# Recurrent attention and slot mixture of experts on one core: guarded GpSimd products, unnormalised slot inputs, a new order

## The chip, the core and the metric

The kernel runs on one core of a Trainium2 chip. The core has five engines that run beside each other and wait for one another by semaphores: PE (TensorE, matrix products into PSUM, its weight loads listed as PEld), DVE (VectorE), ACT (ScalarE), POOL (GpSimd, which also issues most loads here) and SP (which issues the output). Sixteen DMA engines move data between HBM and SBUF. The metric is the device time of one execution in microseconds (us).

## What is computed

Two layers in a row. The first is a recurrent attention: for each of 4 batches and 8 heads (768 tokens, head width 48) a state of 48 x 48 decays by `w` and takes in the product of key and value at each token. The second mixes all 3072 tokens (width 384) into 32 slots, sends 4 slots to each of 8 experts, and mixes the results back.

```python
for t in range(S):
    cur = np.einsum('bhd,bhe->bhde', u[None] * kt, vt)
    y[:, :, t] = np.einsum('bhd,bhde->bhe', rt, state + cur)
    state = w[None, :, :, None] * state + np.einsum('bhd,bhe->bhde', kt, vt)
...
logits = x @ phi                      # x: y with heads side by side, 3072 x 384
d = softmax(logits over tokens)
slot_input = d.T @ x                  # 32 x 384
slot_out[e] = np.maximum(slot_input[e] @ w1[e], 0.0) @ w2[e]
c = softmax(logits over slots)
out = c @ slot_out
```

## The kernel before

The tokens are cut into 6 chunks of 128 (names carry the chunk c, a pair of batches bl, and a half hf of the heads). For each chunk the kernel turns the raw rows of k, r and v into columns on PE, scales them on the way out of PSUM with tables of powers of w, and computes scores, a diagonal term, the output y (kept as x) and the next state.

Every step is a named task of a small planner (`Plan`, L50): it has an engine, a function, other tasks that must stand ahead of it, and the PSUM banks and buffers that it takes. The table ORDER (L13) lists the tasks in the order in which they are emitted, with the bank numbers behind a colon and, behind a slash, the engine (D, A or P for DVE, ACT, POOL) where there is a choice. Since each engine executes its instructions in the order in which they were emitted, the table sets the order on every engine at once.

The names that matter here:

- `qk`, `qr`, `qv` (L48): a copy of the raw rows into a padded buffer rp, from SBUF to SBUF. `tk`, `tr`, `tv` (L355): transposes on PE. `ek`, `er`, `ev` (L365, or a copy at L201 or L203): eviction, for k and r times a table.
- `bk`, `bv`, `kn`, `vn`: transposes back and their eviction. `A` and `M` (L394, L400): scores on PE, masked on DVE. `pr` (L407): product of k and r; `D`, `ds`: its sums per head. `dv` (L424), on POOL: v times ds. `s`, `S`: state. `Y`, `x`: the output of the recurrence. `X`, `xT`, `l`, `lg`: its transpose and the logits.
- `mx`, `sb`, `ex`, `c`, `cT`: maximum, difference, exponential and transposes for the softmax over slots. `rs`, `rr` (L656): its sums per token and their reciprocals, used when the output is evicted.
- For the softmax over tokens the chunks form three groups g (0 to 2, 3 and 4, 5): `gm`, `gt`, `gr`, `gq`, `gd`, `gb`, `gx` find a running maximum, `gs` subtracts it, `ge` takes the exponential, `dp` (L612) multiplies with x on PE. `gf`, `gg`, `am` give the factor by which the earlier sum `acc` is scaled, `acc` (L616) adds the new one. A row of acc holds the sums of the weights.
- `rc`, `un` (L659, L663): the reciprocal of these sums, and the normalised slot inputs in a padded layout. `h` (L682): products with w1, in two groups of four experts and two halves of the width; `hs` (L691, L693) applies the maximum with zero. `ht`, `hT`: transposes of h. `o` (L709): products with w2, one expert after another, all summed in the bank SO.
- The last expert's w2 comes in two pieces, `Va7` and `Vb7`: with YL = 3 the second has 3 of 8 rows. The first four output tiles don't wait for it: they take what SO holds after the first piece (`so1`), and `gG`, `gE`, `pg` (L762) add the missing rows' part straight from h. The other 20 tiles take `so2`, the whole sum. `p` (L754) is a tile's product, `oe` (L771 on ACT, L773 on DVE) its eviction, `dm` the output transfer of one or several tiles.

Loads are issued from POOL's queue, in among its products: `iL` (36 half pieces of k, r and v), `iW` (8 times w1), `iV` (w2). From the eleventh load on, each waits until the load eight places earlier has landed. They turn float32 into bfloat16 on the way; the first chunk's keys are loaded as float32, one half from SP's queue and one from ACT's.

## Time and profile before

| | us |
|---|---|
| median of 3 runs | 120.48 |
| lowest and highest | 118.22, 120.67 |
| the profiled execution | 118.51 |
| its span, first to last instruction | 116.7 |
| busy in the span: PE, DVE, ACT, POOL | 97.1, 93.4, 75.9, 66.1 |

All times on a row of the profile are those of the profiled execution, counted from the span's start. A row of the timeline has the start, the length, the engine, the line and what is written from what; "x8" says that eight alike stand together, and a bracket tells how long the engine was idle before and what ended the wait. A matmul's end is modelled, so a busy PE isn't a PE at its peak.

### The profile page before, as it was taken

Reading aid. Unit: us, or ns where it says so; the run is one execution under the profiler, and the core shown is the slowest. Engines: PE = TensorE matmul, PEld = TensorE weight load, DVE = VectorE, ACT = ScalarE, POOL = GpSimd, SP = SyncE. Lnnn points to the kernel's source line nnn. Section 1 sums busy time; section 2 is a strip of 40 time slices with the busy share of each in tenths; the row PEclk is TensorE's granted clock in tenths of the full one; section 3 lists DMA queues with packets and bytes.
Section 4 is the critical chain, followed back from the end, with each engine's and each line's share of the span. In section 5 each row is a group of like instructions: output and inputs, shape, how many; then the busy total and the mean of one; then the engine's idle time right before and its main releaser. Section 6 shows DMA issues by size and latency. Waiting matters only on the chain.

```text
span 116.7 us, 3848 instructions
## 1 busy us (share of the span) xinstructions
PE 97.1 (83%) x1624; PEld 75.0 (64%) x1624; DVE 93.4 (80%) x187; ACT 75.9 (65%) x118; POOL 66.1 (57%) x84
## 2 busy tenths in 40 slices
PE   4829999897999999999979999899889959898000
PEld 0329989686988897889958989677564425442000
DVE  6967899999989999999899999997873650299300
ACT  3877399998996899788977872388551060279000
POOL 6935554999899958999998799951210000000000
PEclk9999999999999999999999999999996799999975
DMA  2999999999999999999999999999999993059994
GB/s 34 299 203 207 205 209 206 208 208 206 205 208 218 220 213 216 217 216 208 219 216 215 212 217 215 208 221 216 217 217 211 211 205 66 0 213 394 415 415 181
DMA packets 8992, 25.06 MB, mean 215 GB/s; under 512 B 1168, under 2 KB 5776, under 8 KB 8976
## 3 DMA queue, kind: packets, MB, share of 16 engines
q0 software_dynamic: 7344, 19.27, 84.8%
q1 hardware_dynamic: 1464, 5.16, 11.6%
q10 hardware_dynamic: 168, 0.40, 1.0%
q8 instruction: 12, 0.20, 0.6%
q14 instruction: 4, 0.03, 0.1%
HBM read 39.38 MB, written 4.72 MB: 378 GB/s over the span
## 4 chain that ended last, share of the span: by engine, by line
PE 45%; DVE 30%; issue 7%; DMA 5%; ACT 4%; POOL 1%; ACTq 1%; DVEq 1%; POOLq 0%
DVE AT L400 11%; PE pG L355 10%; PE pG L376 7%; DMA w_all<-in_k_dram 5%; DVE S L453 5%; PE pA L394 4%; PE pG L682 3%; PE pG L754 2%; PE pG L495 2%; PE pG L709 2%; DVE rT L365 2%; PE pG L475 2%; PE pG L469 2%; DVE kT L365 2%; DVE w_all L773 2%
## 5 line engine op out<-in xcount | busy, mean ns | idle before, releaser
L400 DVE TENSOR_TENSOR AT<-pA,mask 128x1024 bf16<-128x1024 f32 x24 | 29.2, 1217 | 0.7 <-PE pA L394 0.6
L201 ACT COPY rp<-raw 128x1536 bf16<-128x1536 bf16 x14 | 20.7, 1487 | 2.8 <-PE pG L355 2.3
L355 PE MATMUL pG<-ident,rp 128*128 128x128 bf16 x288 | 20.7, 230 | 2.1 <-ACT rp L201 2.1
L424 POOL TENSOR_TENSOR dv<-vn,ds 128x768 bf16<-128x768 bf16 x12 | 17.7, 1482 | 4.8 <-ACT ds L201 3.6
L355 PEld LDWEIGHTS <-rp 128*128 128x128 bf16 x288 | 18.1, 103 | 3.0 <-ACT rp L201 2.4
L407 POOL TENSOR_TENSOR pr<-kT,rT 128x1024 bf16<-128x1024 bf16 x8 | 17.1, 2142 | 0.1
L201 ACT CAST x<-pG 128x384 bf16<-128x384 f32 x20 | 9.3, 490 | 4.7 <-PE pG L477 2.6
L394 PE MATMUL pA<-rT,kT 64*128 64x128 bf16 x192 | 9.8, 218 | 1.2 <-DVE AT L400 1.1
L453 DVE TENSOR_TENSOR S<-pG,W 128x384 bf16<-128x384 f32 x20 | 10.4, 547 | 0.0
L201 ACT COPY vT<-pG 128x1024 bf16<-128x1024 bf16 x10 | 10.0, 1023 | 0.5 <-PE pG L355 0.4
L475 PE MATMUL pG<-vn,AT 128*128 128x48 bf16 x192 | 8.7, 183 | 0.0
L773 DVE TENSOR_SCALAR w_all<-pG,rcs 128x384 f32<-128x384 f32 (+1 forms) x13 | 6.9, 596 | 2.2 <-ACT w_all L771 2.2
L394 PEld LDWEIGHTS <-kT 64*128 64x128 bf16 x192 | 5.9, 94 | 4.2 <-issue 3.0
L365 DVE TENSOR_TENSOR kT<-pG,Tk 128x1024 bf16<-128x1024 bf16 x12 | 8.0, 682 | 0.6 <-ACT Tk L309 0.6
L365 DVE TENSOR_TENSOR rT<-pG,Tr 128x1024 bf16<-128x1024 bf16 x12 | 8.1, 683 | 0.3 <-PE pG L355 0.3
L213 POOL DMA_DIRECT2D raw<-in_r_dram x12 | 6.5, 557 | 2.6 <-DMA raw<-in_k_dram 1.8
L213 POOL DMA_DIRECT2D raw<-in_v_dram x12 | 6.3, 531 | 3.0 <-DMA raw<-in_r_dram 3.0
L477 PE MATMUL pG<-dv,ident 128*128 128x384 bf16 x24 | 7.7, 323 | 0.0
L771 ACT ACTIVATE w_all<-pG,rcs 128x384 f32<-128x384 f32 (+1 forms) x12 | 5.8, 586 | 2.7 <-PE pG L762 2.3
L475 PEld LDWEIGHTS <-AT 128*128 128x128 bf16 x192 | 7.1, 96 | 0.2 <-issue 0.2
L201 ACT COPY xT<-pG 128x768 bf16<-128x768 bf16 x7 | 5.6, 800 | 2.5 <-PE pG L495 2.5
L376 PE MATMUL pG<-ident,kT 128*128 128x128 bf16 x80 | 6.2, 237 | 0.9 <-DVE kT L365 0.9
(134 smaller groups left out, 211.6 us busy)
## 6 DMA issues: line engine op xcount, KB each, us to landing
w_all<-in_moe_w_dram POOLq DMA_DIRECT2D x8, 768.0 KB, 19.4
raw<-in_moe_w_dram POOLq DMA_DIRECT2D x7, 768.0 KB, 26.6
out_dram<-w_all SPq DMA_DIRECT2D x5, 768.0 KB, 5.0
raw<-in_r_dram POOLq DMA_DIRECT2D x12, 192.0 KB, 7.1
raw<-in_v_dram POOLq DMA_DIRECT2D x12, 192.0 KB, 7.2
raw<-in_k_dram POOLq DMA_DIRECT2D x10, 192.0 KB, 7.1
raw<-in_moe_w_dram POOLq DMA_DIRECT2D x1, 480.0 KB, 24.4
w_all<-in_k_dram SPq DMA_DIRECT2D x1, 384.0 KB, 4.4
```

The source lines that it names most:

```text
L201: O(act.copy(dst, src))
L213: O(pool.dma_start(out=raw_t(x)[:, bb * JJ * D:(bb + 1) * JJ * D], in_=src[c, bb]))
L355: O(pe.transpose(o[:, :, j, :], rp_r[W[rp]][:, jh * JH + j].rearrange("p b d -> p (b d)"), ident[:]))
L365: O(dve.tensor_mul(dst, src, (Tk, Tr)[which][:, None, jh].to_broadcast(BC)))
L376: O(pe.transpose(bank_b(kb)[:, h * C:(h + 1) * C], src[:, bl, h].rearrange("p a x -> p (a x)"), ident[:]))
L394: O(pe.matmul(pA[:, bb, h4 * C:(h4 + 1) * C], kt[s, bl, h].rearrange("p a x -> p (a x)"), rt[s, bl, h].rearrange("p a x -> p (a x)"), star ...
L400: O(dve.tensor_mul(AT_r[W[f"AT{key}"]][:], pA[:].rearrange("p bb (h t) -> p bb h t", t=C), mask[:, None, None, :].to_broadcast([128, 2, H ...
L407: O(op(e).tensor_mul(pr_r[W[f"pr{c}"]][:, bl], kT_r[W[f"kT{c}"]][:, bl].rearrange("p h j x -> p h (j x)"), rT_r[W[f"rT{c}"]][:, bl].rearra ...
L424: O(op(e).tensor_mul(dv_r[W[f"dv{c}{bl}"]][:], vn_r[W[f"vn{c}{bl}"]][:], ds_r[W[f"ds{c}"]][:, bl, :, :, None].to_broadcast([128, H, 2, D])))
L453: O(dve.tensor_mul(S_r[W[new]][:, s], bank(kb[hf])[:, 0:HD].rearrange("p (h b d) -> p h b d", b=2, d=D), W128[:, s, :, None].to_broadcast( ...
L475: O(pe.matmul(o[:, z:z + D], AT_r[W[at]][:, bb, h4, :], vn[:, hf * H2 + h4, bb, :], start=(c == 0 and h4 == 0 and bb == 0), stop=False, sk ...
L773: O(dve.tensor_scalar(out=dst, in0=src, scalar1=rcs[:, i:i + 1], scalar2=None, op0=ALU.mult))
```

## The change

Eight things are done at once.

1. *Waits of POOL's products.* While emitting, the planner remembers the last DVE instruction of a kind in SHARED (copies of raw rows, products and differences with two SBUF inputs). A task of a kind in HELD that goes to POOL then gets a wait for that instruction (`after`).
2. *Slot inputs unnormalised.* For the last group `un` writes acc plus the bank's new part straight into the padded layout; only the row of sums is added as `acc`. The sums are turned by four small products (`rv`), their reciprocal `hsc` (`rw`) scales h in `hs`.
3. *Start.* Other order of the first loads and settings: POOL makes the index table, the identity and the padding of rp ahead of its first load; DVE no longer sets rp; phi is loaded ahead of u. The keys' two halves come from SP and ACT, as they did.
4. *The first output tile in two banks* (p0a, p0b), so that its halves are evicted from different banks; `so1` is one copy.
5. *Two rows in the last piece of w2* (YL = 2).
6. *Output pieces* of 1, 1, 1, 1, 2, 2 tiles, then 4, 4, then 8.
7. *Extra products* (WARM): 19 products of ones into the scores' bank, behind six named tasks.
8. *A new ORDER*, with other engines for many evictions.

```diff
+WARM = [("gl1", 2), ("gb2", 3), ("dp2", 2), ("o50", 3), ("o60", 6), ("o70", 3)]
+SHARED = ("qk", "qr", "qv", "pr", "dv", "sb", "gd", "gs", "gf", "am")
+HELD = ("pr", "dv", "sb", "gs", "gf", "am")
-zt1 zc iL6 zt3 ze1 iL7 zw:0 zt0 qk00:0/A iL8 za ze3 iL9 zb zt2 qk01:/A iL10 zd:/D ze2 tk00:0,0 ze0 tk01:1 qr0:1/D
...
+zt3 zc iL6 zt1 ze3 iL7 zw:0 zt0 ze1 iL8 zb ze0 iL9 zt2 qk00:0/A za zd:/D ze2 qk01:/D iL10 tk00:0,0 tk01:1 qr0:1/A
...
+        shared = None
         for token in order.split():
...
-            t["fn"](letter.get(e, t["eng"]))
+            e = letter.get(e, t["eng"])
+            t["fn"](e)
+            kind = name.rstrip("0123456789")
+            if e == "DVE" and kind in SHARED and name != "gs2":
+                shared = self.last
+            elif e == "POOL" and kind in HELD and shared is not None:
+                self.after(self.last, shared)
...
+    P = Plan(POOLS)
     def O(ins):
+        P.last = ins
...
+    def after(ins, earlier):
+        tc.add_manual_dep(ins.ins, earlier.ins.name, mybir.DependencyInfo(
+            mybir.DependencyClass.Sync, mybir.DependencyReason.DATA), reason="shared port")
...
-    P = Plan(POOLS)
+    P.after = after
...
-    for bb, eng in enumerate((sp, act)):
-        O(eng.dma_start(out=k0[:, bb * JJ * D:(bb + 1) * JJ * D], in_=k_src[0, bb]))
-    O(sp.dma_start(out=u_r[:, :, 0:D], in_=u[:, None, :].to_broadcast([H, 2, D])))
+    for bb, q in ((0, sp), (1, act)):
+        O(q.dma_start(out=k0[:, bb * JJ * D:(bb + 1) * JJ * D], in_=k_src[0, bb]))
...
+    O(dve.memset(ident_f[:], 0.0))
     for t in (w_r, u_r):
...
-    O(dve.memset(ident_f[:], 0.0))
-    load_rkv(2)
...
+    O(sp.dma_start(out=u_r[:, :, 0:D], in_=u[:, None, :].to_broadcast([H, 2, D])))
+    O(pool.iota(it_i.rearrange("p (j y) -> p j y", j=JJ), pattern=[[-1, JJ], [-JJ, RR]], base=C - 1,
+                channel_multiplier=0))
...
+    for t in rp_r:
+        O(pool.memset(t[:, :, :, D:], 0.0))
+    load_rkv(2)
...
-    O(pool.iota(it_i.rearrange("p (j y) -> p j y", j=JJ), pattern=[[-1, JJ], [-JJ, RR]], base=C - 1,
-                channel_multiplier=0))
...
-    for t in rp_r:
-        O(dve.memset(t[:, :, :, D:], 0.0))
...
-    YL = 3
+    YL = 2
...
-        def mg(e):
-            a = acc[:].rearrange("p m s -> p (m s)")
-            if g:
-                O(dve.tensor_add(a, a, bank(kd)[:, 0:(nM + 1) * ES]))
-            else:
-                O(dve.tensor_copy(a, bank(kd)[:, 0:(nM + 1) * ES]))
-        P.add(f"acc{g}", "DVE", mg, deps=[f"dp{g}"] + ([f"am{g}"] if g else []), use=[kd])
+        if not last:
+            def mg(e):
+                a = acc[:].rearrange("p m s -> p (m s)")
+                if g:
+                    O(dve.tensor_add(a, a, bank(kd)[:, 0:(nM + 1) * ES]))
+                else:
+                    O(dve.tensor_copy(a, bank(kd)[:, 0:(nM + 1) * ES]))
+            P.add(f"acc{g}", "DVE", mg, deps=[f"dp{g}"] + ([f"am{g}"] if g else []), use=[kd])
+        else:
+            for q in range(2):
+                def un(e, q=q):
+                    o = 4 * Spe * q
+                    src = bank(kd)[:, 0:nM * ES].rearrange("p (m s) -> p m s", m=nM)[:, :, o:o + 16]
+                    O(dve.tensor_add(
+                        uns[:, :, q, o:o + 144].rearrange("p m (j x) -> p m j x", x=32 + Spe)[:, :, :, 0:Spe],
+                        acc[:, 0:nM, o:o + 16].rearrange("p m (j x) -> p m j x", j=EG),
+                        src.rearrange("p m (j x) -> p m j x", j=EG)))
+                P.add(f"un{q}", "DVE", un, deps=[f"dp{g}", f"am{g}", "zu"], use=[kd])
+            P.add(f"acc{g}", "DVE", lambda e: O(dve.tensor_add(acc[:, nM, :], acc[:, nM, :],
+                                                               bank(kd)[:, nM * ES:(nM + 1) * ES])),
+                  deps=[f"dp{g}", f"am{g}"], use=[kd])
...
-    csr = sb.tile([128, ES], f32, name="csr")
+    hsc = sb.tile([128, 1], f32, name="hsc")
...
-    P.add("rc", "DVE", lambda e: O(dve.reciprocal(csr[:], acc[:, nM, :])), deps=[f"acc{nG - 1}"])
-    for g in range(2):
-        def un(e, g=g):
-            o = 4 * Spe * g
-            O(op(e).tensor_mul(
-                uns[:, :, g, o:o + 144].rearrange("p m (j x) -> p m j x", x=32 + Spe)[:, :, :, 0:Spe],
-                acc[:, 0:nM, o:o + 16].rearrange("p m (j x) -> p m j x", j=EG),
-                csr[:, o:o + 16].rearrange("p (j x) -> p j x", j=EG)[:, None].to_broadcast([128, nM, EG, Spe])))
-        P.add(f"un{g}", "DVE" if g == 0 else "POOL|DVE", un, deps=["rc", "zu"])
+    def turn_sums(e):
+        for j in range(EG):
+            O(pe.matmul(bank("rvb")[32 * j:32 * j + 32, 0:1], acc[0:1, nM, :], ident_f[0:1, 0:1], start=True, stop=True,
+                        skip_group_check=True))
+    P.add("rv", "PE", turn_sums, deps=[f"acc{nG - 1}"], take=[("rvb", "G")])
+    P.add("rw", "DVE", lambda e: O(dve.reciprocal(hsc[:], bank("rvb")[:, 0:1])), deps=["rv"], use=["rvb"])
...
                 if e == "ACT":
-                    O(act.activation(out=dst, in_=src, func=AF.Relu))
+                    O(act.activation(out=dst, in_=src, func=AF.Relu, scale=hsc[:]))
...
-                    O(dve.tensor_scalar(out=dst, in0=src, scalar1=0.0, scalar2=None, op0=ALU.max))
-            P.add(f"hs{g}{a}", "ACT|DVE", ev, deps=[f"h{g}{a}"], use=[kb])
+                    O(dve.tensor_scalar(out=dst, in0=src, scalar1=hsc[:], scalar2=0.0, op0=ALU.mult, op1=ALU.max))
+            P.add(f"hs{g}{a}", "ACT|DVE", ev, deps=[f"h{g}{a}", "rw"], use=[kb])
...
         P.add(f"gG{y}", "PE", lambda e, y=y, kb=kb: O(pe.matmul(
-            bank(kb), h_sb[1][96:128, nF - YL + y, :], cT[96:128, 0:NE, 0:128], start=True, stop=True)),
+            bank(kb)[:, 0:NE * 128], h_sb[1][96:128, nF - YL + y, :], cT[96:128, 0:NE, 0:128], start=True, stop=True)),
...
-        P.add(f"gE{y}", "ACT|DVE", lambda e, y=y, kb=kb: copy(e, gG[:, y], bank(kb)), deps=[f"gG{y}"], use=[kb])
+        P.add(f"gE{y}", "ACT|DVE", lambda e, y=y, kb=kb: copy(e, gG[:, y], bank(kb)[:, 0:NE * 128]), deps=[f"gG{y}"], use=[kb])
...
             if y0:
-                for x, e_, m0 in (("a", "ACT", 0), ("b", "DVE", Dm // 2)):
-                    P.add(f"so1{x}", e_, lambda e, m0=m0: copy(e, so1[:, m0:m0 + Dm // 2], bank(SO)[:, m0:m0 + Dm // 2]),
-                          deps=[prev], use=[SO])
+                P.add("so1", "DVE", lambda e: copy(e, so1, bank(SO)[:, 0:Dm]), deps=[prev], use=[SO])
...
-                         deps=[f"hT{g}", ld, prev] + (["so1a", "so1b"] if y0 else []), take=[(SO, "G")] if e == 0 else [],
+                         deps=[f"hT{g}", ld, prev] + (["so1"] if y0 else []), take=[(SO, "G")] if e == 0 else [],
...
-    P.add("so2", "DVE", lambda e: copy(e, so2[:], bank(SO)[:, 0:Dm]), deps=[prev], use=[SO])
+    P.add("so2", "ACT|DVE", lambda e: copy(e, so2[:], bank(SO)[:, 0:Dm]), deps=[prev], use=[SO])
...
-    i, last = 0, None
-    for g, sizes in ((0, [1, 1, 2, 4]), (1, [4, 4]), (2, [4, 4])):
+    i, last, pp, pgs = 0, None, [], []
+    for g, sizes in ((0, [1, 1, 1, 1, 2, 2]), (1, [4, 4]), (2, [8])):
...
-                def f(e, g=g, j=j, kb=kb, first=first):
-                    O(pe.matmul(bank(kb)[:, 0:Dm], cT[:, j, g * 128:(g + 1) * 128], so1 if first else so2[:],
-                                start=True, stop=not first))
-                P.add(f"p{i}", "PE", f, deps=(["so1a", "so1b"] if first else ["so2"]) + [f"p{i - 1}" if i else None] + cts,
-                      take=[(kb, "G")])
-                done = f"p{i}"
-                if first:
-                    def f2(e, i=i, kb=kb):
-                        for y in range(YL):
-                            O(pe.matmul(bank(kb)[:, 0:Dm], gG[:, y, i * 128:(i + 1) * 128],
-                                        w2_of(E - 1)[:, nF - YL + y, :], start=False, stop=(y == YL - 1)))
-                    done = P.add(f"pg{i}", "PE", f2, deps=[f"p{i}", f"Vb{E - 1}", f"pg{i - 1}" if i else None] +
-                                 [f"gE{y}" for y in range(YL)], use=[kb])
-                halves = [(0, Dm, "")] if i else [(0, Dm // 2, "a"), (Dm // 2, Dm, "b")]
-                for m0, m1, x in halves:
-                    def ev(e, i=i, kb=kb, m0=m0, m1=m1):
-                        dst, src = obuf[:, i * Dm + m0:i * Dm + m1], bank(kb)[:, m0:m1]
+                halves = [("a", 0, Dm // 2), ("b", Dm // 2, Dm)] if i == 0 else [("", 0, Dm)]
+                for hn, m0, m1 in halves:
+                    def f(e, g=g, j=j, kb=kb + hn, first=first, m0=m0, m1=m1):
+                        O(pe.matmul(bank(kb)[:, 0:m1 - m0], cT[:, j, g * 128:(g + 1) * 128],
+                                    (so1 if first else so2[:])[:, m0:m1], start=True, stop=not first))
+                    pp.append(P.add(f"p{i}{hn}", "PE", f, deps=["so1" if first else "so2"] + pp[-1:] + cts,
+                                    take=[(kb + hn, "G")]))
+                    if first:
+                        def f2(e, i=i, kb=kb + hn, m0=m0, m1=m1):
+                            for y in range(YL):
+                                O(pe.matmul(bank(kb)[:, 0:m1 - m0], gG[:, y, i * 128:(i + 1) * 128],
+                                            w2_of(E - 1)[:, nF - YL + y, m0:m1], start=False, stop=(y == YL - 1)))
+                        pgs.append(P.add(f"pg{i}{hn}", "PE", f2, deps=[f"p{i}{hn}", f"Vb{E - 1}"] + pgs[-1:] +
+                                         [f"gE{y}" for y in range(YL)], use=[kb + hn]))
+                    def ev(e, i=i, kb=kb + hn, m0=m0, m1=m1):
+                        dst, src = obuf[:, i * Dm + m0:i * Dm + m1], bank(kb)[:, 0:m1 - m0]
                         if e == "ACT":
...
-                    names.append(P.add(f"oe{i}{x}", ("ACT", "DVE")[x == "b" or i % 2], ev, deps=[done, "rr"], use=[kb]))
+                    names.append(P.add(f"oe{i}{hn}", "DVE" if hn == "b" or i % 2 else "ACT", ev,
+                                       deps=[(pgs if first else pp)[-1], "rr"], use=[kb + hn]))
...
+    turn_ = ["p0a", "p0b", "p1", "pg0a", "pg0b", "pg1", f"o{E - 1}{nF - YL}", "p2", "pg2", "p3", "pg3", "p4"]
+    for a, b in zip(turn_, turn_[1:]):
+        P.by[b]["deps"].append(a)
     for e in range(E):
...
+    n = 0
+    for after, count in WARM:
+        for x in range(count):
+            P.add(f"F{n}", "PE", lambda e: O(pe.matmul(pA[:, 0, :], ones[:, 0:128], ones[:], start=True, stop=True)),
+                  deps=[after, f"F{n - 1}" if n else None])
+            n += 1
...
```

On POOL the program's start reads so before (raw is the buffer of the loads, w_all here the index table, ident_f the identity):

```order
L213 DMA raw<-in_r_dram 128x1x768
L242 ISA
L242 AFFINE_SELECT ident_f<-ident_f 128x128
L213 DMA raw<-in_r_dram 128x1x768
L245 IOTA w_all 128x128
L213 DMA raw<-in_v_dram 128x1x768 x2
```

and so after:

```order
L262 ISA
L262 IOTA w_all 128x128
L264 AFFINE_SELECT ident_f<-ident_f 128x128
L267 MEMSET rp_77 128x32x16
L267 MEMSET rp_78 128x32x16
L234 DMA raw<-in_r_dram 128x1x768 x2
L234 DMA raw<-in_v_dram 128x1x768 x2
```

Four instructions now stand ahead of the first load.

On POOL, around the first product dv, with the semaphores that each row waits for (DVE_49 is DVE's, Activation_49 ACT's, DMASW those of loads), before:

```order
L213 DMA raw<-in_r_dram 128x1x768 [waits DMASW2_49]
L213 DMA raw<-in_r_dram 128x1x768 [waits DMASW3_49]
L424 TENSOR_TENSOR dv_88<-vn_82,ds_86 128x768 [waits Activation_49]
L213 DMA raw<-in_v_dram 128x1x768 [waits DMASW4_49]
L213 DMA raw<-in_v_dram 128x1x768 [waits DMASW5_49]
```

and after:

```order
L234 DMA raw<-in_v_dram 128x1x768 [waits DMASW4_49]
L445 TENSOR_TENSOR dv_88<-vn_82,ds_86 128x768 [waits DVE_49,Activation_49]
L234 DMA raw<-in_v_dram 128x1x768 [waits DMASW5_49]
L234 DMA raw<-in_k_dram 128x1x768 [waits DMASW6_49]
L234 DMA raw<-in_k_dram 128x1x768 [waits DMASW7_49]
L234 DMA raw<-in_r_dram 128x1x768 [waits DMASW0_49]
```

The product stands one load later and also waits for DVE; the loads behind it wait with it.

On DVE, from the last difference to the slot inputs and h (kT and rT are reused for h and its transpose), before:

```order
L593 TENSOR_TENSOR dd<-lg_all,pG_67 128x128
L588 COPY run_181<-pG_67 128x32
L599 TENSOR_TENSOR fac_189<-run_180,run_181 128x32
L203 COPY cT<-pG_69 128x32x16
L619 TENSOR_TENSOR acc<-acc,pG_68 128x128
L659 RECIPROCAL csr<-acc 128x32
L663 TENSOR_TENSOR uns<-acc,csr 128x3x4x4 x2
L657 RECIPROCAL rcs<-pG_64 128x24
L693 TENSOR_SCALAR kT_71<-pG_65 128x8x64
```

and after:

```order
L609 COPY run_181<-pG_68 128x32
L614 TENSOR_TENSOR dd<-lg_all,pG_68 128x128
L624 TENSOR_TENSOR acc<-acc,fac_189 128x128
L656 TENSOR_TENSOR acc<-acc,pG_64 128x32
L651 TENSOR_TENSOR uns<-acc,pG_64 128x3x4x4 x2
L701 RECIPROCAL hsc<-pG_67 128x1
L727 TENSOR_SCALAR kT_71<-pG_69,hsc 128x8x64
L727 TENSOR_SCALAR kT_70<-pG_65,hsc 128x8x64
```

The factor fac_189 goes to POOL and the scaling of acc comes from POOL to DVE; the copy cT and the reciprocals rcs have left this place.

## What I expect

> **What bounds the kernel now.** I read the stretches first (columns: the stretch in us, busy us and instructions of PE, PEld, DVE, ACT, POOL, then the granted clock, the DMA engines' share, GB/s).
>
> ```profile
> 8.00:80.00 72.00, 68.98 (x1311) 60.16 (x1312) 69.39 (x114) 57.51 (x82) 58.99 (x66) 1.00 1.09 212
> 84.90:88.30 3.40, 2.76 (x67) 2.27 (x63) 2.65 (x12) 1.45 (x4) 0.46 (x1) 1.00 1.04 215
> 88.30:91.70 3.40, 3.32 (x32) 1.25 (x36) 0.88 (x4) 0.60 (x1) 0.00 (x0) 0.50 1.05 217
> ...
> 4.00:94.00 90.00, 83.70 (x1511) 68.51 (x1511) 81.98 (x151) 65.87 (x99) 63.27 (x75) 0.98 1.09 214
> ...
> 102.00:105.00 3.00, 2.89 (x17) 1.43 (x16) 3.00 (x6) 2.21 (x5) 0.00 (x0) 1.00 0.55 204
> 105.00:115.00 10.00, 2.47 (x11) 0.80 (x9) 3.87 (x8) 3.18 (x7) 0.00 (x0) 0.86 1.01 409
> ```
>
> Two things run in parallel. From 8 to 80 us DVE (69.39 of 72) and PE (68.98) leave hardly a gap; that is the chain of waits. But the DMA engines are full from 4 to 94 us as well: the loads stream at 214 GB/s. 105 to 115 is output at 409 GB/s. So I asked when the last weights land and who takes them, in the DMA issues (size, us to landing), the timeline and the chain (start, length, what).
>
> ```profile
> raw<-in_moe_w_dram POOLq DMA_DIRECT2D x1, 480.0 KB, 24.4
> raw<-in_moe_w_dram POOLq DMA_DIRECT2D x1, 288.0 KB, 22.1
> ```
> ```profile
> 73.09 0.59 POOL L219 DMA_DIRECT2D raw<-in_moe_w_dram  x1
> 76.79 0.59 POOL L219 DMA_DIRECT2D raw<-in_moe_w_dram  x1
> ```
> ```profile
> 96.18 2.79 PE pG L709 x61
> 99.00 0.37 DVE vT L203
> 99.39 0.33 ACT vT L201
> 99.76 0.81 PE pG L754 x4
> 100.57 0.50 PE pG L762 x3
> 101.09 0.43 ACT w_all L771
> 101.55 0.94 DVE w_all L773 x2
> ```
> ```profile
> 102.04 7.66 SPq L778 DMA_DIRECT2D out_dram<-w_all  x8
> ```
>
> The last expert's first piece (5 rows of w2) lands at 73.09 + 24.4 = 97.5, its last (3 rows) at 76.79 + 22.1 = 98.9. The products with w2 (L709) begin at 96.18 and end at 98.97. Compute is thus only some 1.2 us behind the weights: had it been early, the five products on the 97.5 piece (5 x 2.79/61 = 0.23) would have ended near 97.75. The serial tail follows: two halves of so1 one after the other, four tiles, three corrections, two halves of tile 0 one after the other, first output issued at 102.04. From there to the span's end at 116.7 it is 14.66 us, nearly all transfer.
>
> **The change part by part.** *Start.* POOL used to issue its first load at once; now iota, select and two memsets of rp stand ahead of it.
>
> ```profile
> 1.25 0.70 POOL L213 DMA_DIRECT2D raw<-in_r_dram  x1 [0.81 <-POOLq L801]
> 1.37 0.62 ACTq L233 DMA_DIRECT2D w_all<-in_k_dram  x1
> 2.82 0.31 POOL L245 IOTA w_all<- 128x128 int32 x1
> 52.81 0.89 POOL L325 MEMSET uns<- 128x960 bf16 x1
> 7.36 0.83 ACT L201 CAST rp<-w_all 128x768 bf16<-128x768 f32 x1 [0.75 <-DMA w_all<-in_k_dram]
> ```
> ```profile
> w_all<-in_k_dram ACTq DMA_DIRECT2D x1, 384.0 KB, 6.0
> raw<-in_r_dram POOLq DMA_DIRECT2D x12, 192.0 KB, 7.1
> ```
>
> Iota and select cost some 0.3 each, a memset of 512 elements 0.89 x 512/960 = 0.47: the first load is issued 0.3 + 0.3 + 0.9 = 1.6 later. That is not a loss of 1.6 in the stream: today the second half of the keys (issued 1.37, landed 7.4) shares the engines with those loads; alone it should land near 6, and what the r loads give up the keys take. I put the stream's end 0.1 late (bounds: 0.3 early, 1.6 late) and the first transposes 1.0 early (0 to 1.7). The two key queues themselves are the same as before.
>
> *Middle.* The table moves evictions. Groups of DVE (count | busy us, mean ns):
>
> ```profile
> L203 DVE COPY xT<-pG 128x768 bf16<-128x768 bf16 x5 | 2.8, 551 | 0.4 <-PE pG L495 0.4
> L203 DVE COPY kn<-pG 128x768 bf16<-128x768 bf16 x5 | 2.7, 548 | 0.2 <-PE pG L376 0.2
> L203 DVE COPY rp<-raw 128x1536 bf16<-128x1536 bf16 x3 | 1.8, 592 | 0.0
> L203 DVE COPY vT<-pG 128x1024 bf16<-128x1024 bf16 x2 | 1.4, 681 | 0.0
> L203 DVE COPY cT<-pG 128x512 bf16<-128x512 bf16 x3 | 1.3, 418 | 0.3 <-PE pG L530 0.3
> ```
>
> DVE loses four kn, two vn of the same width, three xT, three cT: 2.2 + 1.1 + 1.7 + 1.25 = 6.2 us. It gains three rp (1.8), two vT (1.4), one cast of half of the keys (at most ACT's 0.83) and some small subtractions, about 4.2 together. Net 2.0 less on the fullest engine; ACT, with 14 of 72 us free, takes it. Since PE is as full, I count 1.0 (0 to 2.0).
>
> *The waits on POOL.* pr, dv and the subtractions now wait for the last earlier DVE copy or two-input operation. What they guard against is seen once:
>
> ```profile
> 82.56 0.72 POOL L593 TENSOR_TENSOR dd<-lg_all,run 128x256 f32<-128x256 f32 x1 [0.89 <-DVE run L588]
> 82.61 0.72 DVE L599 TENSOR_TENSOR fac<-run,run 128x32 f32<-128x32 f32 x1
> 86.39 0.19 DVE L599 TENSOR_TENSOR fac<-run,run 128x32 f32<-128x32 f32 x1
> 29.84 1.08 POOL L213 DMA_DIRECT2D raw<-in_r_dram  x2
> 30.12 0.66 DVE L203 COPY rp<-raw 128x1536 bf16<-128x1536 bf16 x1
> ```
>
> The same fac takes 0.72 under a POOL operation that began just before it and 0.19 alone: it ended when POOL's did. So the guard's worth is at most a few such 0.5 us, and that fac moves to POOL. Its cost: behind a waiting product stand POOL's loads, and behind dv the y products, x and logits. The loads are covered: 7.1 us from issue to landing at 192 KB per 0.9 us (214 GB/s) means a queue some eight deep, so only a hold of over 6 us leaves the engines idle. For dv I take nothing, with 2 us of delay as the far end.
>
> [...]
>
> *Slot inputs.* The sum, the reciprocal and the products give way to a small sum and two sums straight from PSUM; the scaling goes into the evictions of h.
>
> ```profile
> 87.41 0.30 DVE acc L619
> 87.73 0.36 DVE csr L659
> 88.12 0.22 DVE uns L663
> ```
> ```profile
> 88.38 4.41 PE L682 MATMUL pG<-w_all,uns 128*32 128x512 bf16 x48 [0.23 <-DVE uns L663]
> ```
>
> Of 0.97 us from 87.41 to 88.38 a small acc (0.2 to 0.3) and one uns stay: 0.4 saved. The turned sums and their reciprocal (some 0.4 by csr's row) hide behind h, whose first bank takes a quarter of L682, over 0.6 us even at full clock. The last chunk's c5, cT5 and the row sums move behind h; who waits for them is the gating product and the output tiles, and the wait for weights covers their 1 to 2 us; without that cover they would cost about 1.
>
> *Fillers.* From 88.38 to 91.7 h ran at clock 0.50, 3.3 us; at full clock that is 1.7 shorter. Seven fillers stand ahead of it; whether they hold the clock is open (0 to 1.7 saved). Each costs 0.20 to 0.27 (from 0.81/4 for 384 columns). Nine more, 2.0 us, stand between the last experts' products, hidden only while PE waits for weights.
>
> *Sum of the compute side.* 1.0 + 1.0 + 0.4 + 1.7 = 4.1 us earlier at 96.18, so 92.1; 56 products (2.6) and the nine fillers (2.0) end by 96.7, ahead of the last expert's landing at 98. So the weights bind, with 1.4 us in hand, and of the 4.1 only 1 is paid out.
>
> *Tail.* The first piece now has 6 rows, so it lands at 98.9 - 1.4 x 2/3 = 98.0, with 0.1 of stream 98.1. Six products to 98.4; so1 in one copy of 0.55 (L203's mean for this width) to 99.0, under which three fillers run (up to 0.8, so PE may be free only at 99.2); two tiles' products 0.4, to 99.55; the halves of tile 0 lie in two banks and take two corrections of half width each, 0.25, to 99.8; ACT's half 0.43, DVE's half beside it and 0.2 later, to 100.45; issue at 100.55, against 102.04: 1.5 earlier. The output then is 3072 x 384 x 4 bytes = 4.72 MB. Between 102 and 105 it moved 0.61 MB where 2.1 us at 409 GB/s after a 0.9 lag would be 0.86: 0.6 us lost, of which four single rows regain perhaps 0.2. The single last piece of 8 rows cannot start before all rows are evicted, under 7.7 us after the first issue (the eight issues of today lie within 7.66); the 16 rows before it, 0.197 MB each, need 16 x 0.48 = 7.7 us of transfer after a 0.9 lag, so the engines are still busy: nothing, at worst 0.5. Sum: 1.7 us. The profiled execution took 118.51 (span 116.7 and 1.8 around it), so 116.8; it stood 2.0 under the median of 120.48, near the lowest of 118.22.
>
> **Rivals.** (1) *The clock falls while PE waits for weights.* In 88.3 to 91.7 it was 0.50 after a stretch in which PE was busy for 2.76 of 3.40 us. Once the weights bind, PE has 2 us of gaps between 92 and 98; at half clock the three fillers take 1.4 instead of 0.7 and the first tiles 1.2 instead of 0.8: +1.1, 117.9. [...] (2) *The stream starts 1.6 late* because the keys regain nothing: everything from 98.1 on moves by 1.5, 118.3. (3) *Slower: POOL's waits and the new order stall the middle.* DVE has twice as many rp copies; one that finds a running pr waits it out as fac did (2.14 us at most, a row of the groups), and a held dv delays y.
>
> ```profile
> L407 POOL TENSOR_TENSOR pr<-kT,rT 128x1024 bf16<-128x1024 bf16 x8 | 17.1, 2142 | 0.1
> ```
>
>  Then the nine fillers lie on the path: the balance is 4.1 won and 0.9 in the tail (two banks, one so1, corrections) against 2.0 of fillers, so it decides from 3.0 us, three or four holds of a us. At 6 us of holds the end is 3.0 late, 121.5. Against it: in the trace POOL's products meet DVE's copies nowhere long, and loads do not starve. (4) *The new order wins nothing:* compute arrives as late as before, the fillers cost 2.0 and the tail gives 0.9: 119.6.
>
> **Numbers.** Forecast 0.48, (1) 0.18, (2) 0.10, (3) 0.13, (4) 0.11. About 2% (2.4 us) is what a measurement of this kernel can tell from no change: the executions before lie 2.4 apart. Against the median the line is 118.1; a median that falls among the slower executions, as 120.48 did, adds up to 2 to any case. Two thirds of the forecast and half of (1) fall below it: 0.32 + 0.09 = 0.41 faster. Slower by 2% of either yardstick takes (3) almost whole, 0.12 with a tail of (4); the rest is 0.47. Range: down to 115.2 (stream 0.3 early and 0.1 not late, the 6-row piece 0.4 sooner, the other 0.4 of the output's loss regained, and 0.3 as the lowest execution lay below the profiled one), up to 119.9 ((4), and (1) or (2) in a slower execution); outside lie most of (3) and a tenth of the rest.
>
> **What would show it.** Right: PE has gaps before the last w2 products and they follow the landing of the 6-row piece near 98; first output near 100.5; output at about 409 GB/s without the dip after it. The start is right if the first transposes begin near 7.2 and the loads still end at 99. The clock in h shows the fillers. Wrong: L709's successor ending later than 98.9 with no wait on a load (rival 3 or 4), DVE copies over 1 us, a load stream ending after 100, or a clock of 0.50 between 96 and 101.

## The result, and the profile after

| | before | after |
|---|---|---|
| median, lowest, highest (13 executions each) | 119.01, 118.18, 121.11 | 117.50, 117.09, 118.05 |
| profiled execution, its span | 118.51, 116.7 | 117.38, 115.6 |

The ratio is 0.9919, interval 0.9891 to 0.9947: about 0.8% faster, a gain that 2% cannot tell from no change. All ratios leave out executions over 1.5% above the fastest of the same kernel, here the six of before at 120.48 or more, and two of the three shown at the outset were of these.

The stretches of after, with the columns of those of before:

```profile
8.00:80.00 72.00, 68.43 (x1315) 60.01 (x1316) 68.07 (x112) 57.27 (x85) 59.43 (x66) 1.00 1.09 212
88.30:91.70 3.40, 3.40 (x59) 1.83 (x58) 1.71 (x4) 1.36 (x2) 0.00 (x0) 1.00 1.06 219
101.30:104.30 3.00, 2.92 (x18) 1.49 (x17) 2.27 (x5) 2.77 (x6) 0.00 (x0) 1.00 0.65 231
102.00:105.00 3.00, 2.88 (x16) 1.35 (x14) 2.50 (x5) 2.93 (x7) 0.00 (x0) 1.00 0.89 319
105.00:115.00 10.00, 1.84 (x9) 0.58 (x7) 3.37 (x7) 2.42 (x6) 0.00 (x0) 0.78 0.92 376
```

DVE has 1.3 us less work between 8 and 80 (69.39 before), and h runs at clock 1.00. From 102 to 105 the output moves 319 GB/s against 204, but mostly because it began earlier: in the first 3 us from its first issue it is 231, so most of the dip is still there. Next the timeline at the start, the loads of the last expert, and the end of the chain of waits:

```profile
7.11 0.24 PE L335 MATMUL pA<-ident_f,u_r 8*128 8x8 f32 x1 [1.54 <-ACT rp L222]
9.07 0.56 DVE L224 CAST rp<-w_all 128x768 bf16<-128x768 f32 x1
9.78 2.51 PE L376 MATMUL pG<-ident,rp 128*128 128x128 bf16 x22 [2.43 <-DVE rp L224]
73.67 0.59 POOL L240 DMA_DIRECT2D raw<-in_moe_w_dram  x1
79.34 0.59 POOL L240 DMA_DIRECT2D raw<-in_moe_w_dram  x1
88.20 2.77 PE L716 MATMUL pG<-w_all,uns 128*32 128x512 bf16 x48
101.32 7.45 SPq L811 DMA_DIRECT2D out_dram<-w_all  x9
```
```profile
raw<-in_moe_w_dram POOLq DMA_DIRECT2D x1, 576.0 KB, 25.0
raw<-in_moe_w_dram POOLq DMA_DIRECT2D x1, 192.0 KB, 20.3
```
```profile
94.06 2.06 PE pG L743 x48
96.12 0.75 PE pA L826 x3
96.88 0.44 PE pG L743 x8
97.32 1.40 PE pA L826 x6
98.72 0.03 issue
98.75 0.50 PE pG L743 x6
99.25 0.75 PE pA L826 x3
100.00 0.38 PE pG L788 x3
100.38 0.66 PE pG L795 x6
```

The first transposes came 1.5 later than before (9.78 against 8.24), not earlier. The products with w2 (L743) began 2.1 earlier (94.06). The fillers (L826) ended at 98.72, just as the 6-row piece landed (73.67 + 25.0 = 98.7); the first output was issued 0.7 earlier than before (101.32).

### The profile page after: what moved, and what is told of

It reads as the page before. It is cut to its first block, busy times and chain, and to the rows that moved or that the text cites. A ratio compares the mean times of both kernels' runs of the same rounds, so it can differ in the third digit from the quotient of the medians.

```text
span 115.6 us, 3911 instructions
## 1 busy us (share of the span) xinstructions
PE 98.7 (85%) x1649; PEld 76.0 (66%) x1649; DVE 89.8 (78%) x178; ACT 76.7 (66%) x124; POOL 66.4 (57%) x85
## 4 chain that ended last, share of the span: by engine, by line
PE 48%; DMA 17%; DVE 11%; ACT 9%; POOL 5%; issue 3%; DVEq 0%; ACTq 0%; POOLq 0%
DMA w_all<-in_moe_w_dram 17%; PE pG L376 9%; PE pA L415 4%; PE pG L788 3%; ACT rp L222 3%; PE pG L397 3%; PE pA L826 3%; PE pG L743 3%; PE pG L633 2%; PE pG L716 2%; PE pG L516 2%; PE pG L551 2%; POOL w_all L237 2%; PE pG L490 2%; PE pG L496 2%
## 5 line engine op out<-in xcount | busy, mean ns | idle before, releaser
L376 PE MATMUL pG<-ident,rp 128*128 128x128 bf16 x288 | 22.5, 235 | 2.6 <-DVE rp L224 2.4
L376 PEld LDWEIGHTS <-rp 128*128 128x128 bf16 x288 | 19.2, 106 | 3.8 <-issue 2.8
L222 ACT COPY rp<-raw 128x1536 bf16<-128x1536 bf16 x11 | 16.3, 1479 | 2.6 <-PE pG L376 2.3
L222 ACT COPY vT<-pG 128x1024 bf16<-128x1024 bf16 x8 | 8.0, 1015 | 5.2 <-PE pG L376 5.2
L222 ACT CAST x<-pG 128x384 bf16<-128x384 f32 x19 | 8.5, 487 | 0.8 <-PE pG L498 0.5
L222 ACT COPY xT<-pG 128x768 bf16<-128x768 bf16 x10 | 8.0, 804 | 1.3 <-PE pG L516 1.2
L222 ACT COPY vn<-pG 128x768 bf16<-128x768 bf16 x10 | 8.0, 815 | 0.9 <-PE pG L397 0.9
L222 ACT COPY kn<-pG 128x768 bf16<-128x768 bf16 x9 | 7.3, 812 | 0.5 <-PE pG L397 0.5
```

What stands on the lines that cost most here:

```text
L222: O(act.copy(dst, src))
L376: O(pe.transpose(o[:, :, j, :], rp_r[W[rp]][:, jh * JH + j].rearrange("p b d -> p (b d)"), ident[:]))
```

## Experiments

Each kernel is the kernel before or after with one edit. Ratios go against runs of before on the same chip.

| kernel | median (lowest to highest) | ratio, interval |
|---|---|---|
| after, no waits on POOL | 122.34 (117.64 to 122.60) | none: one execution would be left |
| before, waits alone | 118.94 (118.33 to 121.31) | 1.0031, 1.0003 to 1.0059 |
| after, no fillers | 119.42 (119.09 to 119.63) | 1.0073, 1.0043 to 1.0103 |
| after, tiny fillers | 118.14 (117.12 to 119.75) | 0.9967, 0.9930 to 1.0004 |
| before, 7 fillers | 120.71 (119.90 to 121.72) | 1.0175, 1.0113 to 1.0236 |
| before, 7 fillers, 7 warming products less | 118.91 (117.87 to 119.20) | 1.0023, 0.9987 to 1.0059 |
| before, 14 tiny products more | 119.62 (118.96 to 122.08) | 1.0074, 1.0039 to 1.0109 |
| before, 34 tiny products more | 118.80 (118.22 to 121.69) | 1.0019, 0.9994 to 1.0044 |
| after, old start | 117.26 (117.03 to 117.47) | 0.9896, 0.9869 to 0.9924 |
| after, u ahead of phi | 117.22 (116.89 to 118.23) | 0.9904, 0.9868 to 0.9939 |
| after, first load ahead | 118.34 (117.75 to 118.89) | 0.9986, 0.9961 to 1.0010 |
| after, old start, three fillers tiny | 117.16 (116.82 to 117.50) | 0.9906, 0.9872 to 0.9940 |

### What the waits on POOL are worth

After without them:

```diff
-                self.after(self.last, shared)
+                pass
```

> The changed kernel without the waits of POOL's products for DVE's copies, all else alike. Theory (the weights' landing and the fillers between the last experts' products set the end, the middle has over 1 us in hand): the time stays within 0.3 us of the changed kernel's 117.5, the last 6-row piece lands at 98.7 as it does there and its six products start at 98.75. Rival (the waits are what gained): 0.8 us or more slower, 118.3 or above, with DVE copies stretched towards 2 us by running POOL products and the w2 products starting after 94.8 instead of 94.0.

Five of six executions took 122.0 to 122.6, one 117.64. The timeline of DVE and POOL in the profiled one, and DVE's groups in after:

```profile
14.36 2.36 POOL L428 TENSOR_TENSOR pr<-kT,rT 128x1024 bf16<-128x1024 bf16 x1 [0.47 <-DVE rT L386]
14.66 2.62 DVE L428 TENSOR_TENSOR pr<-kT,rT 128x1024 bf16<-128x1024 bf16 x1
```
```profile
L224 DVE COPY rp<-raw 128x1536 bf16<-128x1536 bf16 x6 | 3.3, 552 | 0.0
L428 DVE TENSOR_TENSOR pr<-kT,rT 128x1024 bf16<-128x1024 bf16 x4 | 2.7, 682 | 0.0
L428 POOL TENSOR_TENSOR pr<-kT,rT 128x1024 bf16<-128x1024 bf16 x8 | 17.0, 2130 | 5.1 <-DVE rT L386 4.6 <-DVE pr L428 0.3
```

A product of 0.68 took 2.62: it ended only after POOL's, which had begun 0.3 ahead. In after POOL waits, and neither DVE group is stretched (552 and 682 ns). Without the waits both are:

```profile
L428 DVE TENSOR_TENSOR pr<-kT,rT 128x1024 bf16<-128x1024 bf16 x4 | 5.9, 1469 | 0.0
L224 DVE COPY rp<-raw 128x1536 bf16<-128x1536 bf16 x6 | 4.1, 682 | 0.0
```

That is 4.0 us more of DVE's time, and the products with w2 began 4.75 later, at 98.81 instead of 94.06. (In this trace the clock also was 0.50 from 20.5 to 23.9, which it was not in after.)

```profile
98.81 2.06 PE pG L743 x48
```

So in five of six executions the waits carry about 4.8 us in this order, where the expectation had 0.3; no trace shows how the sixth came to 117.64 without them. Of the two `pr` above the one that began second ended second (POOL's 14.36 to 16.72, DVE's 14.66 to 17.28), as `fac` did in before (82.61 to 83.33, beside POOL's 82.56 to 83.28); what the two engines share isn't shown.

Then the same waits alone, in before's order:

```diff
+            if e == "DVE" and kind in SHARED and name != "gs2":
+                shared = self.last
+            elif e == "POOL" and kind in HELD and shared is not None:
+                self.after(self.last, shared)
```

> The kernel before with its own order, and only the waits of GpSimd's products on VectorE's last shared copy or product added. Theory (the waits' worth lies in meetings that happen in some executions and not in others; the executions of before near 120.5 are those in which a VectorE operation met a running GpSimd product): all executions at 118.0 to 119.0, none above 119.6, and the lowest as before's lowest to 0.4. Rival 1 (before's two groups of times come from elsewhere, for instance from the output's transfers): a third or more of the executions still above 119.6. Rival 2 (in before's order the waits hold GpSimd and cost): all executions above before's lowest by 0.8 or more.

No worth and at most 0.7 us of cost there. In that order the two engines hardly met: before's trace has DVE's four `pr` at 708 ns, near the 682 of after. Its two issues of loads at 29.84 took 0.54 each beside DVE's copy at 30.12, as others do (531 to 593 ns on the mean). And five of twelve executions still took 120.1 to 121.3, so rival 1 holds: the spread of before's times is something else. The profile caught one of these longer executions, and its stretches show a candidate:

```profile
86.90:93.70 6.80, 6.52 (x86) 2.86 (x83) 2.96 (x9) 0.60 (x1) 0.39 (x1) 0.50 1.04 214
97.20:100.50 3.30, 3.30 (x50) 1.74 (x44) 0.00 (x0) 0.00 (x0) 0.00 (x0) 0.50 0.15 29
```

The clock was 0.50 for 6.8 us about h, and again in the products with w2. In the profiled execution of before it was 0.50 once ahead of the output, for 3.4 us. The mean clock of each execution goes with this: 0.935 to 0.950 in all those of before above 120, 0.952 to 0.966 in all but one of the others. But the two ranges all but touch, so that the clock makes the whole difference isn't shown.

### What the fillers are worth

After without any of the 19 (WARM empty, and F0 to F18 gone from ORDER):

```diff
-WARM = [("gl1", 2), ("gb2", 3), ("dp2", 2), ("o50", 3), ("o60", 6), ("o70", 3)]
+WARM = []
```

> The changed kernel without any of the 19 extra products. Theory: h runs at half clock again and takes 4.4 instead of 2.8 us, so the w2 products start near 95.6 instead of 94.0; but without nine fillers (2.1 us) among them the six products of the 6-row piece still start at its landing near 98.7, and the first tiles start 0.15 sooner because three fillers no longer stand in front of them: 117.3 to 117.6, no slower than the changed kernel. Rival (the fillers carry the gain): 118.3 or above, with the first output issued at 102 or later. Second rival (PE's clock falls to half while it waits for the weights): granted clock 0.5 between 96 and 101, first output 0.8 later, 118.2.

1.9 us slower than after. The first output was issued only 0.5 later (101.79), so the rest is in the output; its stretches:

```profile
86.80:93.60 6.80, 5.94 (x72) 2.40 (x71) 2.51 (x8) 1.12 (x3) 0.25 (x1) 0.50 1.05 216
105.00:115.00 10.00, 2.27 (x11) 0.76 (x8) 3.84 (x8) 2.88 (x7) 0.00 (x0) 0.78 0.97 392
115.00:117.50 2.50, 0.00 (x0) 0.00 (x0) 0.00 (x0) 0.00 (x0) 0.00 (x0) 0.50 0.04 15
```

For its last us or so packets went one at a time, as from one of the 16 DMA engines alone (share 0.04 in the last row, 15 GB/s). Next, before with the seven fillers that stand ahead of h:

```diff
+    for after, count in (("gl1", 2), ("gb2", 3), ("dp2", 2)):
```

> The kernel before with seven extra products alone, two, three and two of them behind gl1, gb2 and dp2, where the changed kernel has them. Theory (the kernel before was 1.2 us behind its weights because h ran at half clock): h at full clock takes 2.8 instead of 4.4 us, the w2 products start near 94.6, the 5-row piece's products end near 97.8 instead of 98.97 and the time falls by 1.0 to 1.2 us against the kernel before, ratio 0.990 to 0.992, as much as the whole change. Rival (the gain of the change lies in its tail, two banks and small first pieces): less than 0.4 us, ratio above 0.997.

The profiled execution kept its clock at 1.00 from 11.7 to 110.7, and its first output was issued at 101.66, 0.4 earlier than before; still it was 1.75% slower. The end of its chain and the same stretch behind 115:

```profile
73.34 24.70 DMA raw<-in_moe_w_dram
98.05 0.04 issue
98.09 0.50 PE pG L709 x5
```
```profile
115.00:117.50 2.50, 0.00 (x0) 0.00 (x0) 0.00 (x0) 0.00 (x0) 0.00 (x0) 0.50 0.04 17
```

In both kernels the output had something else beside it. The page's list of DMA queues counts fetches of instructions, here of before and of this kernel:

```profile
q8 instruction: 12, 0.20, 0.6%
```
```profile
q8 instruction: 13, 0.21, 0.7%
```

The trace's DMA records place each: one packet of 16 KB, on average for every 243 to 251 of TensorE's weight loads and matmuls. The 13th came, by kernel, when 3242 to 3255 of these had started; before, with 3248 in all, never asks for it, so the count gives the place only to about a dozen. While the 13th ran inside an output, mostly 15 packets of the output were under way at a time, and 16 afterwards: by this it takes one engine's place. The records don't tell the engines apart; that the late packets are those of the same engine is inferred.

### Is it the place of the fetch?

Three kernels part the number of instructions from the fillers' work. After with fillers of 4 columns:

```diff
-pA[:, 0, :], ones[:, 0:128], ones[:]
+pA[:, 0, 0:4], ones[:, 0:128], ones[:, 0:4]
```

> The changed kernel with all 19 fillers still there, but 4 columns wide instead of 512: the number of TensorE instructions is kept, the work is gone. Theory (without fillers the time grew from 117.5 to 119.4 for two reasons, h at half clock, and a fetch of TensorE instructions that fell into the output): h at clock 0.5 again, 4.4 to 5.2 us, products with w2 ending near 99.4, first output issued 101.6 to 102.0, the fetch ahead of the output, the last outputs landing at one go; 117.7 to 118.3. Rival (the clock alone cost the 1.9 us): 119.2 to 119.7. Second rival (the waits between instructions, not the work, hold the clock): h at 2.8 us and 117.0 to 117.5.

118.14, with the clock at 0.50 from 87.0 to 93.8, and the fetch at 102.0, ahead of the output: as the theory had it, though the first output was issued at 102.29, later than expected. So of the 1.9 us, 1.3 come back with the number of instructions alone. The 0.6 that are left to after's 117.50 would be the fillers' work, but the two intervals overlap. The 7 fillers in before again, and the 7 warming products of the program's start left out:

```diff
-    fill(3)
...
-    fill(4)
```

> The kernel before with 7 fillers in front of h, as in the earlier run of that kind (120.71), and the 7 warming matmuls of the program's start left out, so that TensorE has as many instructions as before. Theory (the 7 fillers gain 0.4 to 0.8 by the clock, and lost it only because TensorE's 13th fetch of instructions fell into the output): no fetch after 93 us, first output issued 101.4 to 101.9, no slow tail of the output, 117.4 to 118.2 (ratio to before's lower group 0.990 to 0.997). Rival (the fillers themselves, or the earlier output, bring the slow tail): 119.9 or more. A start 0.5 later at low clock would move either up by as much.

The slow tail of the output is gone, and 1.8 us of the 120.71 with it. The gain of 0.4 to 0.8 did not come in the median, though. The ten executions part by their mean clock: 117.87 to 118.31 in the four at 0.972 or more, 118.83 to 119.20 in the six at 0.963 to 0.965. Stretches of the profiled execution (119.04) between h and the output:

```profile
92.00:95.40 3.40, 2.09 (x31) 1.15 (x32) 1.69 (x3) 1.99 (x3) 0.00 (x0) 1.00 1.05 212
95.40:98.80 3.40, 3.40 (x48) 1.82 (x44) 0.00 (x0) 0.00 (x0) 0.00 (x0) 0.50 0.60 116
```

PE was busy for 2.09 of 3.40 us behind h, and the next 3.4 us, those of the w2 products, ran at half clock. After has nine more fillers there, and PE is busy throughout (that these nine keep the clock is argued, not shown: no run leaves out them alone):

```profile
93.40:96.80 3.40, 3.40 (x66) 1.75 (x63) 0.31 (x1) 0.87 (x2) 0.00 (x0) 1.00 1.00 200
```

The purest form is before with nothing but instructions added: 14 tiny products behind the transpose of u, then 20 more where PE waits for hT.

```diff
+            O(pe.matmul(pG[0][:, 0:4] if n == 14 else pA[:, 0, 0:4], ones[:, 0:128], ones[:, 0:4], start=True, stop=True))
...
-zw:0
+zw:0 f:14
...
-ht0:3
+ht0:3 f:20
```

> The kernel before, and nothing more than 14 matmuls of 4 columns put behind the transpose of u, where TensorE idles. Theory (TensorE's 13th fetch of instructions comes when some 3254 of its weight loads and matmuls have started, and one DMA engine then gives its part of the output late): with 28 more the fetch lands near 104 to 105.5, in the output; first output issued as before (102.0), its last transfer ends 1.3 to 2 later than 115.3; executions in two groups, the lower at 119.6 to 120.4, the upper near 122. Rival (a fetch in the output is harmless; the slow output came from the fillers' wake or the earlier output): the lower group at 118.2 to 118.8, as before.

> As the run with 14 tiny matmuls, with 20 more of them where TensorE waits for the transposed h. Theory (place of the fetch): 68 more instructions bring the fetch to about 100, ahead of the output, and the time back: lower group 118.2 to 118.8, output at 409 GB/s to its end. Rival (each added instruction, or the 13th fetch wherever it lies, costs): as with 14 or more, 119.6 up.

With 14 the fetch came at 104.5, with 34 at 101.2. The same stretch of the output, first with 14, then with 34:

```profile
105.50:106.50 1.00, 0.85 (x5) 0.34 (x4) 1.00 (x3) 1.00 (x3) 0.00 (x0) 1.00 0.35 126
```
```profile
105.50:106.50 1.00, 0.85 (x5) 0.38 (x4) 1.00 (x3) 1.00 (x4) 0.00 (x0) 1.00 0.95 378
```

The direction is the theory's and the size about half: 0.7% slower, and back with 20 more. The trace's records of the output (first byte to last) and of the 13th fetch, over the profiled executions:

```
fetch (start, us)                    output takes
none:  before, waits alone,
       7 fillers and 7 less          12.4 12.4 12.4
ahead: after 100.9 (output 102.2)    12.0
       old start, u ahead, first load 12.3 12.3 12.0
       old start + three tiny        12.1
       no waits, tiny fillers        12.2 12.0
       34 tiny 101.2 (output 103.2)  12.4
inside: 14 tiny 104.5 (1.5 us long)  13.2
        no fillers 105.1 (1.7)       13.8
        7 fillers 105.3 (1.9)        14.3
```

All eleven with the fetch outside the output need 12.0 to 12.4 us, the three with it inside 13.2 to 14.3, with one trace for each kernel.

### The start

After with the loads and settings of before's start:

```diff
+    O(sp.dma_start(out=u_r[:, :, 0:D], in_=u[:, None, :].to_broadcast([H, 2, D])))
...
+    load_rkv(2)
     O(sp.dma_start(out=phi_f[:], in_=moe_phi.rearrange("(p mo) s -> p mo s", mo=nM)))
-    O(sp.dma_start(out=u_r[:, :, 0:D], in_=u[:, None, :].to_broadcast([H, 2, D])))
...
-    for t in rp_r:
-        O(pool.memset(t[:, :, :, D:], 0.0))
-    load_rkv(2)
...
+    for t in rp_r:
+        O(dve.memset(t[:, :, :, D:], 0.0))
```

> The changed kernel with the start of the kernel before: POOL's loads ahead of the index table and the identity, rp's padding set by DVE, u loaded ahead of phi. Theory (the load stream, late by 0.8 in the changed kernel, sets the end): the stream ends at 98.9 instead of 99.7, the 6-row piece lands at 97.9 instead of 98.7, the first transposes start near 7.5 instead of 9.8, so PE has passed its fillers by then, the six products start near 97.95 and the first output is issued 0.8 earlier: 116.7 (116.4 to 116.9). Rival (fillers and not the landing hold PE): the six products start at 98.5 or later although the weights have landed by 98, and the time falls by less than 0.3 us.

The 6-row piece landed at 98.35 (97.9 was expected) and the first transposes began at 9.04 (7.5). The six products stood right on the landing, and the first output was issued at 100.97: 0.35 earlier than in after, where 0.8 was expected; the time's interval overlaps that of after. Two halves of this edit: u's load ahead of phi's alone, and the first load ahead of POOL's settings alone.

```diff
+    O(sp.dma_start(out=u_r[:, :, 0:D], in_=u[:, None, :].to_broadcast([H, 2, D])))
     O(sp.dma_start(out=phi_f[:], in_=moe_phi.rearrange("(p mo) s -> p mo s", mo=nM)))
-    O(sp.dma_start(out=u_r[:, :, 0:D], in_=u[:, None, :].to_broadcast([H, 2, D])))
```

> The changed kernel with u's load ahead of phi's on SyncE's queue again; the loads of GpSimd stay as late as in the changed kernel. Theory (the stream's start sets the end, the transposes' start does not): first transposes at 8.2 to 8.8 instead of 9.78, the 6-row piece still landing near 98.7, first output issued near 101.3, 117.3 to 117.6. Rival (the late transposes cost): 117.0 to 117.25, with compute waiting for the weights longer.

The transposes began at 8.19, as expected and 1.6 earlier than in after, but h only 0.4 earlier (88.20 in after):

```profile
87.78 2.77 PE L716 MATMUL pG<-w_all,uns 128*32 128x512 bf16 x48
```

The 6-row piece landed at 98.62 and the first output was issued at 101.24, as the theory had it. The median of 117.22 falls in the rival's range, 0.1 below the theory's; with executions from 116.89 to 118.23 the times can't decide.

```diff
+    load_rkv(2)
     O(pool.iota(it_i.rearrange("p (j y) -> p j y", j=JJ), pattern=[[-1, JJ], [-JJ, RR]], base=C - 1,
                 channel_multiplier=0))
...
-    load_rkv(2)
     load_rkv(3)
```

> The changed kernel with its first three loads on GpSimd's queue ahead of the iota, the select and the memsets again; u's load stays behind phi's. Theory (the stream's start sets the end): first load issued near 1, the 6-row piece landing near 98.35, six products on its landing, first output issued 100.9 to 101.0, 117.1 to 117.3. Rival (the late transposes cost the 0.25): 117.4 to 117.6 with the products ending after the landing by more than their own 0.5.

A miss for both theories: 0.8 us slower than after, with the 6-row piece landing at 100.2. The other loads now came half a us later (the second at 3.48) and the transposes at 10.44. Where the stream broke, POOL's timeline and the following stretch:

```profile
13.24 0.51 POOL L234 DMA_DIRECT2D raw<-in_v_dram  x1 [0.41 <-DMA raw<-in_r_dram]
15.89 2.12 POOL L428 TENSOR_TENSOR pr<-kT,rT 128x1024 bf16<-128x1024 bf16 x1 [2.14 <-DVE pr L428]
17.96 0.56 POOL L234 DMA_DIRECT2D raw<-in_v_dram  x1
```
```profile
20.00:23.00 3.00, 2.85 (x55) 2.66 (x53) 3.00 (x6) 2.74 (x5) 3.00 (x5) 1.00 1.11 168
```

The first product waits 2.14 for DVE's (the guard), and the next load stands behind it: 4.7 us between two issues, and then the stream falls to 168 GB/s. In after, the same hold lasts 2.9 us (14.41 to 17.30) and the same stretch has 205. By 30 us this kernel had loaded 4.83 MB, after 4.98, which is 0.7 us of stream, and it is not made up. That is half of the 1.5 by which the landing is later; where the other half arose isn't shown.

### A last trim

The old start, and the three fillers behind the six products cut to 4 columns:

```diff
-lambda e: O(pe.matmul(pA[:, 0, :], ones[:, 0:128], ones[:], start=True, stop=True))
+lambda e, w=4 if after == "o70" else 512: O(pe.matmul(
+    pA[:, 0, 0:w], ones[:, 0:128], ones[:, 0:w], start=True, stop=True))
```

> The changed kernel with the start of before (117.26 in the earlier run) and the three fillers behind the 6-row products cut to 4 columns; their number is kept. Theory (these three end 0.15 to 0.2 after so1 and hold the first tiles; the fetch of instructions stays near 100.4, ahead of the output): first output issued 100.75 to 100.85, 117.05 to 117.15. Rival 1 (the three are hidden behind so1): 117.2 to 117.35. Rival 2 (they hold the clock; without them it halves behind 98.9): first tiles twice as long, 117.8 or more.

117.16, the lowest median of all, but its interval overlaps that of after: what it gains over after isn't shown. The first output was issued at 101.08, 2.62 behind the landing of the 6-row piece (98.46). With the three at full width it was 2.62 as well (98.35 to 100.97), so they are hidden, as the first rival had it.

## Why the prediction was right or wrong

The forecast of 116.8 was 1.7 below the profiled execution of before; measured were 1.1 below it (117.38), 0.8% by the ratio. The range held it, and so did the likeliest of the three chances (within 2%). The direction stood; the gain came out at about half to two thirds. What failed for the time is the stream's end (0.6 late) and the yardstick; the largest miss, half of the compute sum, hardly shows in the time, because the weights bind.

**The weights bind: right.** In the four kernels of the start and the last trim the six products stand on the landing of their piece, and the first output is issued 2.62 behind it, for landings from 98.35 to 100.19. In after (98.70 to 101.32) it is the same, with the fillers ending at the moment of the landing. That is why 2.1 us of earlier compute paid 0.7 at the first output.

**The compute sum, 4.1: 2.1 came.** h at full clock saved 1.64 of 1.7. The gap lies ahead of it: by start, middle and slot inputs h was to begin 2.4 earlier, and it began 0.2 earlier (88.20 against 88.38). The start was counted 1.0 earlier and was 1.5 later: "the two key queues themselves are the same as before" looked at keys and POOL, and not at u, which now stands behind phi on SP's queue. Its transpose ran at 7.11 and DVE, in order, did the tables behind it before it cast the keys at 9.07. But with u ahead of phi the transposes came 1.6 earlier and h only 0.4. So the larger miss is the assumption that time won in the start or the middle reaches h in full. DVE's 1.3 us less work between 8 and 80 (2.0 were counted) did not bring h forward either. What holds the middle instead stays open. The 1.4 us "in hand" were used up by this: the fillers ended as the piece landed.

**The stream's end: 98.7 instead of 98.1.** This is the term that made the time miss: 0.6, as much as 117.38 lies above 116.8. "I put the stream's end 0.1 late" has two parts. The start moved it by 0.25 to 0.35 (98.35 and 98.46 in the two kernels with the old start), not by 0.1. And the profiled execution of before had landed early: its 5-row piece came at 97.45, where five other traces with that order and start have 97.60 to 98.13. One trace's landing time was taken for the kernel's.

**The tail: right.** From the landing to the first output 2.45 were reckoned, 2.62 measured. In before with the clock held the old tail took 3.6 (98.05 to 101.66). The output regained 0.4 (14.28 from its first issue to the span's end, against 14.66) where 0.2 was counted. The half clock of rival 1 did not come: the clock was 1.00 from 14.9 to 110.5.

**The waits: their cost right, their worth wrong.** "At most a few such 0.5 us" was read from before's trace, whose order keeps the two engines apart; this order doesn't, and without the waits it loses 4.8. Rival 3 had the mechanism (a DVE product that met a running `pr` waited it out: 2.62 for 0.68) and the place, but priced the kernel that holds the waits. And "only a hold of over 6 us leaves the engines idle" gave too much room: behind one of 4.7 us the stream fell from 205 to 168 GB/s, though the engines' share stayed at 1.11 (1.15 in after).

**The fillers: two things missed.** They were counted for h (1.7) and as cover while weights are awaited, both right. Not counted was the clock in the w2 products: rival 1 saw its fall as a danger of after, whereas two traces of before's order have it there, while none of after's 13 executions goes above 118.05; that the nine fillers see to this is argued. And 38 more PE instructions move a fetch, which in after falls 1.3 us ahead of the output's first byte. That is luck: no step of the prediction saw to it, and with the 38 gone again it fell inside.

**The yardstick.** Against the median of 120.48 the forecast meant 3.7 us less, and the chance of faster, 0.41, leaned on that median. Two of its three executions were among the six longer ones; over 13 the median was 119.01, and after's is 1.5 below it.

The slot inputs, the two banks and the output pieces were not tried one by one, so what each of them carries of the 0.8% isn't shown.

## What to carry to other kernels

A guard against two engines blocking each other has to be priced in the order that it guards (here 4.8 us), not in the trace of the old one (at most a few times 0.5), and what queues behind the waiting instruction (here loads) sets how long it may wait (a hold of 4.7 us took the stream from 205 to 168 GB/s). Where two streams end within a us of each other, take landing times from several executions before one of them is called the bound. When instructions are added for the clock's sake, count them: they also shift where the next fetch of instructions meets the transfers (14 tiny products more: at 104.5, inside the output; 34: at 101.2, ahead of it).

## What the runs showed of the hardware that was not expected

- The trace has fetches of instructions of 16 KB each, one for every 243 to 251 of TensorE's weight loads and matmuls; that they are TensorE's is inferred from this, and from the 13th, which came at 104.5 with 14 tiny products added and at 101.2 with 34. By the packets under way (15 of the output in place of 16) a fetch inside the output took the place of one of the DMA engines that move the data. Among the loads it took 0.9 to 1.1 us, just ahead of the output 0.9 to 1.5, and cost nothing that the times show; inside the output it took 1.5 to 1.9, and the output 0.8 to 1.9 us more.
- Ahead of the output the clock was halved for 3.4 or 6.8 us at a time. It halved after stretches in which PE was busy for 2.09 of 3.40 us (above, before with 7 fillers and 7 warming products less) and for 2.76 of 3.40 (before, ahead of h). The same share doesn't always halve it: before with 7 fillers kept 1.00 behind this stretch, as empty as the one above:

```profile
93.60:97.00 3.40, 2.09 (x52) 1.36 (x53) 0.42 (x1) 1.66 (x3) 0.00 (x0) 1.00 0.97 189
```
